# x of the first two tiles split by partitions over two queues, the K weights on ScalarE's queue, and new orders on all engines

## The chip, the cores and the metric

The kernel runs on one core of a Trainium2 chip. Its time is the device time of that core in microseconds (us); the time of a kernel is the median of its runs. A profile is one profiled execution. Engines: PE is TensorE (matmuls; PEld its weight loads), DVE is VectorE, ACT is ScalarE, POOL is GpSimd, SP is SyncE, which here only issues transfers. ACT issues a few transfers too.

## What is computed

A linear-attention block and a gated feed-forward block, each behind a layer norm and with a residual; 2048 rows of width 448, 16 heads of 28, feed-forward width 1792, bf16.

```python
def _A_ref(x, wqkv, wo):
    qkv = (x @ wqkv) ...            # q, k, v of 16 heads of 28
    phi = lambda t: jnp.where(t > 0, t + 1, jnp.exp(t)) + 1e-6
    pq, pk = phi(q), phi(k)
    kv = jnp.einsum("bhsd,bhse->bhde", pk, v)
    z = jnp.einsum("bhsd->bhd", pk)
    num = jnp.einsum("bhqd,bhde->bhqe", pq, kv)
    den = jnp.einsum("bhqd,bhd->bhq", pq, z)[..., None] + 1e-6
    return (num / den) ... @ wo

def _B_ref(x, w_gate, w_up, w_down):
    g = jnp.einsum("bsd,df->bsf", x, w_gate)
    u = jnp.einsum("bsd,df->bsf", x, w_up)
    return jnp.einsum("bsf,fd->bsd", _gelu(g) * u, w_down)

h = x + _A_ref(_layernorm(x), A_wqkv, A_wo)
h2 = h + _B_ref(_layernorm(h), B_w_gate, B_w_up, B_w_down)
```

## The kernel before

The 2048 rows lie in SBUF as 16 tiles of 128: partition p holds rows 16p to 16p+15, tile t is row 16p+t of each (`xv`). So neighbouring tiles of one partition lie side by side in memory.

**Head and K stage.** For each tile DVE takes the statistics (`bnst1_t`, line 413, and `bnag1_t`, line 414), ACT a logarithm and an exponential (`ln1_t`, line 420, and `rstd1_t`, line 422: the reciprocal root of the variance). Tiles 0 to 3 are normalized on DVE (`normD_t`, line 435), transposed on PE (`tr0_t` and `tr1_t`, line 443, two blocks each), and copied back by ACT (`evxA_t`, line 448) and DVE (`evxD_t`, line 450). Tiles 4 to 15 are normalized on POOL (`negm1_t`, `normP_t`, line 453) and transposed by a transfer that SP issues (`xT_t`, line 455). Then PE makes the K tiles and the Q tiles (`k_t`, `q_t`, line 469: four matmuls of 448 columns each, the third and fourth of which also need `dw0_t` or `dw1_t`, the last 64 rows of the weights), ACT and DVE make phi of K (`ek_t`, `ck_t`, `pk_t`, lines 480 to 482), and PE adds pk^T times the normalized rows over all tiles in four banks (`pt...`, line 488; the last columns of xnn hold ones and give z). Before any of this PE runs `warm`: WARM matmuls of 128 columns on a constant (line 407).

**Middle.** The sums in the banks are copied out (lines 514 to 521), multiplied by the V weights (`kv`, line 527), masked to heads, multiplied by wo (`w2_c`, line 547). The remaining Q tiles fill PE meanwhile. Per pair of tiles the denominator is formed (`cq`, `aq`, `t1`, `dr`, `rd`, `pn`, lines 564 to 593), the result is transposed (`tro` on PE for the first pair, `oT_p` as transfers) and multiplied (`out...`), x is added (`hr_t`, line 633), and the second layer norm follows (`nhP_t` on POOL, `wrap_t` on DVE, line 664, and the transfer `hT_t`, line 665).

**Gate and up stage.** In chunks of 2, 2, 4, 4 and 4 tiles PE makes gate and up products (`gu2_v`, `gu4_v`, lines 731 and 733) into a ring of two banks each; ACT takes the gelu (`ge0_v`, `ge1_v`, line 751), DVE the product (`hm0_v`, `hm1_v`, line 753); a unit v+2 needs both products of unit v. The down products (`downA_p`, `downB_p`, line 697; `down448_14`, `down224_15`, line 678) are placed between the units, DVE adds x (`fo...`) and SP stores (`do_t`).

**What sets the order.** Every operation is a task with a number, in the order in which the builder makes it. The order of each engine is written out by hand in `ORDERS`: five lists of task numbers for PE, ACT, DVE, POOL and SP. An engine works strictly along its list. Waits follow from what a task reads and writes. Where a task waits for more than one semaphore, all but the last wait are instructions of their own ahead of it; `HOLD` names, for a task, whose wait stands first. It has 15 entries.

The first transfers are issued in this order: on SP x of tile 0, x of tiles 2 and 3, `dw1` (Q weights, 384 rows), x of tiles 4 to 7, `dw1_t`, the rest of x, then V weights and wo; on ACT x of tile 1, `dw0` (K weights, 384 rows), `dw0_t` (K weights, the last 64 rows), and then the table load `tbl1`.

Of the kernel before, what the change touches and what calls it, by code (L numbers as in the profile page):

```python
# [48 lines left out]
)  # L49
HOLD = {  # L50
    66: (36,), 141: (140,), 165: (164,), 214: (213,), 216: (215,), 323: (302,), 326: (324,), 431: (340,), 704:
    (564,), 735: (734,), 781: (672,), 839: (836,), 849: (846,), 854: (852,), 866: (865,),
}


class _Buf:
    __slots__ = ("name", "writer", "readers")

    def __init__(self, name):
        self.name = name  # L60
        self.writer = None
        self.readers = []

# [165 lines left out]
def bass_sequential_preLN__linear_attn_block__glu_gated_geglu__prompt_kernel(  # L229
# [13 lines left out]
    WARM = 40  # L243
# [579 lines left out]
```

## Time and profile before

| | |
|---|---|
| median of 3 runs | 190.3 us (190.28 to 190.66) |
| span of the profiled execution, first to last instruction | 188.3 us |
| the profiled execution's own time | not recorded; the median is 2.0 us over the span |
| PE busy | 184.3 us (98%) |
| DVE busy | 129.3 us (69%) |
| ACT busy | 76.5 us (41%) |
| POOL busy | 50.0 us (27%) |
| transposes xT, issue to landing | 2.5 to 4.1 us, median 2.7 us |

Busy time is the union of an engine's instructions. The chain of waits follows the work that ended last back through what released it; 94% of it is PE, 3% DVE, 1% transfers. Times inside the span count from its first instruction. An issue row on SPq or ACTq is the time the queue's engine spends on issuing; the landing time is counted from the start of that issue. In a row "L469 PE MATMUL ps<-wqk_sb,xnT ... x8" eight instructions of line 469 that follow each other are merged, with the start of the first and the time to the end of the last.

### The profile page before, as it was taken

Reading aid. Unit: us, or ns where it says so; the run is one execution under the profiler, and the core shown is the slowest. Engines: PE = TensorE matmul, PEld = TensorE weight load, DVE = VectorE, ACT = ScalarE, POOL = GpSimd, SP = SyncE. Lnnn points to the kernel's source line nnn. Section 1 sums busy time; section 2 is a strip of 40 time slices with the busy share of each in tenths; the row PEclk is TensorE's granted clock in tenths of the full one; section 3 lists DMA queues with packets and bytes.
Section 4 is the critical chain, followed back from the end, with each engine's and each line's share of the span. In section 5 each row is a group of like instructions: output and inputs, shape, how many; then the busy total and the mean of one; then the engine's idle time right before and its main releaser. Section 6 shows DMA issues by size and latency. Waiting matters only on the chain.

```text
span 188.3 us, 4459 instructions
## 1 busy us (share of the span) xinstructions
PE 184.3 (98%) x1813; PEld 109.2 (58%) x1813; DVE 129.3 (69%) x330; ACT 76.5 (41%) x220; POOL 50.0 (27%) x91
## 2 busy tenths in 40 slices
PE   7999999999999999999999999999999999999994
PEld 7545555555688788965554555555545545454554
DVE  4999959999899998786796762562645244335432
ACT  3878752799963231432234222321242222224100
POOL 6067910704505686033614000206100000000000
PEclk9999999999999999999999999999999999999999
DMA  5996458999393526820005720000096000002024
GB/s 169 387 231 88 96 104 194 218 222 174 65 320 64 95 52 116 84 52 0 0 3 98 144 54 0 0 3 2 3 135 111 3 0 24 3 0 98 3 79 140
DMA packets 35076, 17.11 MB, mean 91 GB/s; under 512 B 26864, under 2 KB 33648, under 8 KB 35056
## 3 DMA queue, kind: packets, MB, share of 16 engines
q1 hardware_dynamic: 34432, 16.32, 41.1%
q10 hardware_dynamic: 624, 0.52, 0.8%
q8 instruction: 14, 0.23, 0.5%
q14 instruction: 6, 0.05, 0.1%
HBM read 8.26 MB, written 1.84 MB: 54 GB/s over the span
## 4 chain that ended last, share of the span: by engine, by line
PE 94%; DVE 3%; DMA 1%; issue 0%
PE ps L733 38%; PE ps L697 19%; PE ps L469 12%; PE ps L731 9%; PE ps L488 6%; PE ps L627 3%; PE ps L678 3%; PE ps L628 2%; DMA x_sb<-in_A_x_dram 1%; DVE st L413 1%; PE ps L617 1%; PE ps L547 1%; PE ps L527 1%; PE ps L443 0%; PE ps L654 0%; DVE den L572 0%
## 5 line engine op out<-in xcount | busy, mean ns | idle before, releaser
L733 PE MATMUL ps<-hnT,wgu_sb 64*128 64x512 bf16 (+1 forms) x490 | 88.8, 333 | 0.0
L731 PE MATMUL ps<-hnT,wgu_sb 64*128 64x512 bf16 (+1 forms) x490 | 88.6, 333 | 0.0
L751 ACT ACTIVATE gl<-ps 128x256 bf16<-128x256 f32 x112 | 36.6, 383 | 85.3 <-PE ps L731 84.4
L753 DVE TENSOR_TENSOR hh<-ps,gl 128x256 bf16<-128x256 f32 x112 | 42.1, 416 | 41.4 <-ACT gl L751 41.3
L733 PEld LDWEIGHTS ps<-hnT,wgu_sb 64*128 64x128 bf16 x490 | 45.2, 94 | 32.9 <-DVE hh L753 3.4
L731 PEld LDWEIGHTS ps<-hnT,wgu_sb 64*128 64x128 bf16 x490 | 45.4, 94 | 2.5
L697 PE MATMUL ps<-wd_sb,hh 64*128 64x448 bf16 x392 | 41.5, 349 | 0.0
L697 PEld LDWEIGHTS ps<-wd_sb,hh 64*128 64x128 bf16 x392 | 23.2, 94 | 14.5
L469 PE MATMUL ps<-wqk_sb,xnT 128*128 128x448 bf16 x128 | 27.4, 353 | 0.0
L413 DVE BATCH_NORM_STATS2 st<-x_sb 128x6 f32<-128x448 bf16 x32 | 19.2, 612 | 1.8 <-DMA x_sb<-in_A_x_dram 1.7
L585 POOL TENSOR_TENSOR t<-pq,zbc 128x448 f32<-128x448 bf16 x12 | 12.3, 1042 | 23.7 <-DVE pq L583 22.0
L469 PEld LDWEIGHTS ps<-wqk_sb,xnT 128*128 128x128 bf16 x128 | 11.9, 98 | 11.4 <-DVE pk L482 0.8
L488 PE MATMUL ps<-pk,xnn 128*128 128x448 bf16 x64 | 13.9, 352 | 0.0
L627 PE MATMUL ps<-w,pqnT 64*128 64x448 bf16 x49 | 11.5, 349 | 0.1
L425 POOL TENSOR_SCALAR ln<-mv 128x2 f32<-128x2 f32 x7 | 2.0, 291 | 35.2 <-DVE mv L414 35.0
L480 ACT ACTIVATE e<-ps 128x448 bf16<-128x448 f32 x16 | 8.5, 539 | 5.6 <-PE ps L469 5.5
L628 PE MATMUL ps<-pt_sb,pqnT 64*128 64x448 bf16 x42 | 10.2, 350 | 0.0
L633 DVE TENSOR_TENSOR x_sb<-ps,x_sb 128x448 bf16<-128x448 f32 x16 | 9.6, 616 | 0.7 <-PE ps L628 0.6
L662 POOL TENSOR_SCALAR hn<-x_sb,nm,rs 128x448 bf16<-128x448 bf16 x14 | 9.9, 719 | 0.4
L482 DVE SCALAR_TENSOR_TENSOR pk<-ps,e 128x448 bf16<-128x448 f32 x16 | 9.8, 617 | 0.1
L488 PEld LDWEIGHTS ps<-pk,xnn 128*128 128x128 bf16 x64 | 6.3, 98 | 5.9 <-DVE pk L482 0.3
L453 POOL TENSOR_SCALAR xnn<-x_sb,nm,rs 128x448 bf16<-128x448 bf16 x12 | 8.9, 744 | 2.2 <-ACT rs L422 1.9
(85 smaller groups left out, 160.5 us busy)
## 6 DMA issues: line engine op xcount, KB each, us to landing
out_dram<-x_sb SPq DMA_DIRECT2D x15, 112.0 KB, 1.8
wd_sb<-in_B_w_down_dram SPq DMA_DIRECT2D x1, 1568.0 KB, 8.4
x_sb<-in_A_x_dram SPq DMA_DIRECT2D x3, 448.0 KB, 5.9
wgu_sb<-in_B_w_gate_dram SPq DMA_DIRECT2D x1, 896.0 KB, 12.1
wgu_sb<-in_B_w_up_dram SPq DMA_DIRECT2D x1, 896.0 KB, 16.5
wgu_sb<-in_B_w_gate_dram SPq DMA_DIRECT2D x1, 672.0 KB, 6.1
wgu_sb<-in_B_w_up_dram SPq DMA_DIRECT2D x1, 672.0 KB, 8.5
wo_sb<-in_A_wo_dram SPq DMA_DIRECT2D x1, 392.0 KB, 7.5
```

What stands on the lines that cost most here:

```text
L413: op("dve", lambda e: e.bn_stats(st[:, t, :], src_ap), [b_src], [b_st[t]], "bnst%s_%d" % (tag, t))
L469: ins = e.matmul(ps[:, bk, 0:D], xnT[:, t, k, :], wqk_sb[:, k, c0:c0 + D], start=(k == 0), stop=(k == 3))
L488: ins = e.matmul(ps[:, BK_PT[c], 0:D], xnn[:, t % XN_R, c * 128:(c + 1) * 128], pk[:, ip, :], start=(t == 0), stop=(t == T - 1))
L585: op("pool", lambda e, n=n: e.tensor_tensor(t1[:, n, :], pq[:, a + n, :], zbc[:, :], ALU.mult), [b_pq[a + n]] + b_z, [b_t1[n]], "t1p_%d" % ...
L627: e.matmul(ps[:, BK_OUT[0], 0:D], pqnT[ra, i2, sg // 2, :], w2[ra, sg // 2, :], start=(sg == 0), stop=(sg == 5))
L628: ins = e.matmul(ps[:, BK_OUT[1], 0:D], pqnT[rb, i2, 3 + (sg + 1) // 2, :], (w2 if sg == 6 else w2s)[rb, sg // 2, :], start=(sg == 0), sto ...
L662: op("pool", lambda e, t=t, sh=sh: e.tensor_scalar(hn[:, sh, 0:D], x_sb[:, t, :], nm2[:, t:t + 1], rs2[:, t:t + 1], ALU.add, ALU.mult), [b ...
L697: ins = e.matmul(ps[:, bko[half][n], 0:D], hh[rows, j, sl[n]], wd_sb[rows, j, :], start=(j == 0 and (half == 0 or p == 6)), stop=(j == NJ ...
L731: first = e.matmul(psG[:, jj * N:(jj + 1) * N], wgu_sb[A_, k, j * 128:(j + 1) * 128], hnT[A_, ka_, c0:c0 + N], start=(k == 0), stop=(k == ...
L733: ins = e.matmul(psU[:, jj * N:(jj + 1) * N], wgu_sb[B_, k, j * 128:(j + 1) * 128], hnT[B_, kb_, c0:c0 + N], start=(k == 0), stop=(k == NK ...
L751: G.add("act", lambda e, gi=gi, cs_=cs_, psG=psG: e.activation(gl[:, gi, cs_], psG[:, cs_], AF.Gelu_apprx_tanh), r=[b_ps[BK_G[i]]], w=[b_g ...
L753: op("dve", lambda e, dst=dst, srcU=srcU, srcL=srcL: e.tensor_tensor(dst, srcU, srcL, ALU.mult), [b_ps[BK_U[i]], b_glh], [b_ar[j_][t % HR] ...
```

## The change

1. x of tiles 0 and 1 is loaded as one array, split by partitions: partitions 0 to 63 on SP's queue, 64 to 127 on ACT's. The statistics of tiles 0 and 1 wait for both halves.
2. SP then issues `dw0_t`, x of tiles 2 and 3, x of tiles 4 to 7, `dw1_t` and the rest; ACT issues `dw0` and `dw1`, and then the table load.
3. WARM goes from 40 to 36.
4. All five orders are new, and `HOLD` has an entry for nearly every task with a wait.

```diff
-    WARM = 40
+    WARM = 36
...
-        dma_x("sp", 0, 1)
-        dma_x("act", 1, 2)
+        x01 = [dma(q, x_sb[rows, 0:2, :], xv[rows, 0:2, :], b_, "dx0%s" % "ab"[i]) for i, (q, rows, b_) in enumerate((("sp", A_, b_x[0:2]), ("act", B_, [_Buf("x01")])))]
+        dma_w1("sp", wqk_sb, D, 2 * D, b_wk, "dw0_t")
+        dma_w3("act", wqk_sb, D, 2 * D, b_wk, "dw0")
         dma_x("sp", 2, 4)
-        dma_w3("act", wqk_sb, D, 2 * D, b_wk, "dw0")
-        tx1 = dma_w1("act", wqk_sb, D, 2 * D, b_wk, "dw0_t")
-        dma_w3("sp", wqk_sb, 0, D, b_wq, "dw1")
+        tx1 = dma_w3("act", wqk_sb, 0, D, b_wq, "dw1")
         dma_x("sp", 4, 8)
...
         def ln_stats(t, src_ap, b_src, st, mv, b_st, b_mv, tag):
-            op("dve", lambda e: e.bn_stats(st[:, t, :], src_ap), [b_src], [b_st[t]], "bnst%s_%d" % (tag, t))
+            G.add("dve", lambda e: e.bn_stats(st[:, t, :], src_ap), r=[b_src], w=[b_st[t]], name="bnst%s_%d" % (tag, t), sync=x01[1:] if tag == "1" and t < 2 else ())
```

The orders are lists of hundreds of numbers; written as names, these are the places that the prediction speaks of (each list goes on):

```
DVE  before  wvpad wqkpad bnst1_0 bnag1_0 bnst1_1 bnag1_1 normD_0 bnst1_2 normD_1 bnag1_2 bnst1_3 evxD_0 ...
DVE  after   wqkpad bnst1_0 bnst1_1 bnag1_0 wvpad bnag1_1 bnst1_2 normD_0 bnag1_2 normD_1 bnst1_3 evxD_0 ...
PE   before  ... k_1 q_0 tr0_3 tr1_3 k_2 k_3 pt4_0 q_1 pt4_1 pt4_2 q_2 k_4 pt4_3 k_5 q_3 k_6 pt4_4 k_8 pt4_5 k_7 pt4_6 k_10 k_9 ...
PE   after   ... k_1 tr0_3 tr1_3 q_0 k_2 k_3 pt4_0 pt4_1 q_1 k_4 q_2 q_3 pt4_2 k_5 pt4_3 k_6 k_7 pt4_4 pt4_5 k_8 k_9 k_10 ...
ACT  before  ... ln1_8 ek_3 eq_0 ln1_7 rstd1_8 rstd1_7 ...
ACT  after   ... ek_3 ln1_8 rstd1_8 eq_1 rq_1 ln1_7 rstd1_7 ...
PE   before  ... pt1_14 pt1_15 pt3_13 pt3_14 pt3_15 q_5 q_4 kv ...
PE   after   ... pt1_15 pt3_12 pt3_13 pt3_14 pt3_15 q_4 q_5 kv ...
DVE  before  ... evpD_3 z0 aq_1 t1d_0 dr_0 evpD_2 rd_0 ...
DVE  after   ... evpD_3 z0 t1d_0 dr_0 dr_1 evpD_2 ...
DVE  after   ... hm1_9 hm0_9 fo448_0 wrap_7 cqP_6 wrap_4 rdP_5 ...
SP   before  ... hT_4 oT_4 hT_5 hT_7 hT_6 oT_5 ...
SP   after   ... oT_4 hT_5 hT_6 hT_7 hT_4 oT_5 ...
PE   after   ... downB_6 down224_15 down448_14 down224_15
```

POOL's order puts `ident`, `kvzpad` and `ones2` ahead of `eps`, and several other constants behind the first normalizations. Between gate and up units the down products, `fo448`, `wrap` and the stores stand in other places.

More of the change, by code (lines that the diff above doesn't have):

```diff
@@ L15 @@
 ORDERS = (
[33 rows of a table removed]
[33 rows of a table added]
 )
 HOLD = {
-    66: (36,), 141: (140,), 165: (164,), 214: (213,), 216: (215,), 323: (302,), 326: (324,), 431: (340,), 704:
-    (564,), 735: (734,), 781: (672,), 839: (836,), 849: (846,), 854: (852,), 866: (865,),
[77 rows of a table added]
 }
```

143 rows, old and new, of tables (HOLD, ORDERS) are left out of this document.

## The prediction

> **What bounds the kernel now.** I read the page's totals first, then the list of waits of PE, then the chain of waits over the first 16 us.
>
> ```profile
> span 188.3 us, 4459 instructions
> PE 184.3 (98%) x1813; PEld 109.2 (58%) x1813; DVE 129.3 (69%) x330; ACT 76.5 (41%) x220; POOL 50.0 (27%) x91
> ...
> PE ps L443 <- DVE xnn L435: 0.4, 1, 0.4
> ...
> 0.79 2.53 DMA x_sb<-in_A_x_dram
> ...
> 3.34 0.64 DVE st L413
> ...
> 6.09 0.40 PE ps L443 x4
> ...
> 6.88 0.55 PE ps L469 x2
> ...
> 7.65 1.51 PE ps L469 x8
> ```
>
> The span is 188.3 us and the median of the runs 190.3, so 2.0 us lie outside the profiled instructions; I keep them and add the sum to 190.3. Between its first real work and the last 2 us of the span PE is at work: after the warm-up it waits in the list of PE once, for 0.4 us. So nothing on DVE, ACT, POOL or the queues is worth time except what lets PE begin sooner (x lands, DVE takes statistics and normalizes, PE transposes, K0) or closes a small hole. On the other side, anything that comes late for PE is paid in full. The eight matmuls at 7.65 take 1.51 us; a unit of four (one K tile, one Q tile, one "pt" product) is 0.757 us.
>
> **Part 1: the head.** Transfers and issues in the order of landing times and of the queues, then DVE's steps:
>
> ```profile
> x_sb<-in_A_x_dram SPq DMA_DIRECT2D x1, 112.0 KB, 2.5
> x_sb<-in_A_x_dram ACTq DMA_DIRECT2D x1, 112.0 KB, 2.7
> x_sb<-in_A_x_dram SPq DMA_DIRECT2D x1, 224.0 KB, 3.4
> wqk_sb<-in_A_wqkv_dram ACTq DMA_DIRECT2D x1, 336.0 KB, 4.2
> ...
> 0.79 0.87 SPq L346 DMA_DIRECT2D x_sb<-in_A_x_dram  x2
> 1.25 1.01 ACTq L346 DMA_DIRECT2D wqk_sb<-in_A_wqkv_dram  x2
> 1.71 0.43 SPq L346 DMA_DIRECT2D wqk_sb<-in_A_wqkv_dram  x1
> ...
> 4.10 0.59 DVE L413 BATCH_NORM_STATS2 st<-x_sb 128x6 f32<-128x448 bf16 x1
> 4.22 0.29 ACT L420 ACTIVATE ln<-mv,eps_t 128x1 f32<-128x1 f32 x1 [0.65 <-DVE mv L414]
> 4.83 0.36 DVE L435 TENSOR_SCALAR xnn<-x_sb,mv,rs 128x448 bf16<-128x448 bf16 x1
> 5.11 0.62 DVE L413 BATCH_NORM_STATS2 st<-x_sb 128x6 f32<-128x448 bf16 x1
> 6.54 0.27 DVE L450 COPY xnT<-ps 128x256 bf16<-128x256 bf16 x1
> ```
>
> Each half of the new array has the 112 KB of one old tile, in half as many rows of twice the length. Statistics of tile 0 started with tile 0's landing (0.79 + 2.5, at 3.34); now they need both halves. The nearest rows are those two transfers: 2.5 and 2.7 us. Bounds for the start: 3.1 (longer rows gain 0.2) to 3.6; I take the slower old queue, 0.80 + 2.7 = 3.5, which is +0.1 rounded down. Behind the waiting instruction stand all of DVE's head, and through it ACT's logarithms and PE's transposes.
>
> DVE's new order takes both tiles' statistics, then tile 2's, before it normalizes tile 0. Up to the copy of line 450 that releases the second half of K0 (6.54, which is 3.20 after 3.34) the same statistics, aggregates and normalizations stand in another order, plus the pad of wv_sb moved in, about 0.15. The gaps that the old order left for ACT are used, so I count the order itself at nothing (0 to +0.15). But statistics of tile 2 now stand in front of tile 0's normalization, and x of tiles 2 and 3 became the third issue of SP instead of the second: 1.71 instead of about 1.22 (two issues take 0.87). With the old 3.4 us it lands at 5.1; if the engines serve the K weights first (1.25 + 4.2) at 5.45; if it has them to itself at the old 4.6. DVE gets there at 3.45 + two statistics, two aggregates and the pad (0.53 + 0.53 + 0.35) = 4.86. The wait is 0 to 0.6; I take 0.2, the row of the same transfer. Everything behind it on DVE moves with it. Head: +0.1 + 0.2 = **+0.3** (-0.2 to +0.8).
>
> [...]
>
> Priced at nothing: ACT issues three transfers as before, and the logarithm waited 0.65 for DVE, which covers a table load that comes up to that much later; beyond it each 0.1 costs 0.1. The four warm-up matmuls fewer end the warm-up earlier, and the transpose waits for DVE in any case (rival 3 has the other side). POOL's small constants move behind its pads and are needed only at 4.22.
>
> **Part 2: K tiles come earlier on PE.** The new PE order takes K4 two units sooner (before q_2, with pt4_1 ahead of q_1) and K7 three units sooner (straight behind K6). Both read transposes that SP issues one after the other.
>
> ```profile
> L455 SPq DMA_TRANSPOSE xnT<-xnn x1: 1307/1307/1307, 10.3 to 10.3; - x1
> DMA to landing us min/median/max: 3.3/3.3/3.3
> L455 SPq DMA_TRANSPOSE xnT<-xnn x1: 1264/1264/1264, 16.6 to 16.6; - x1
> ...
> 13.80 1.68 PE L469 MATMUL ps<-wqk_sb,xnT 128*128 128x448 bf16 x8
> 20.61 0.92 PE L469 MATMUL ps<-wqk_sb,xnT 128*128 128x448 bf16 x4
> ...
> 13.88 0.33 ACT L422 ACTIVATE rs<-ln 128x1 f32<-128x1 f32 x2
> 14.17 0.75 POOL L453 TENSOR_SCALAR xnn<-x_sb,nm,rs 128x448 bf16<-128x448 bf16 x1 [0.23 <-ACT rs L422]
> ```
>
> The rows at 13.80 are q_2 and K4, so K4 starts at 14.55; two units sooner is 13.04. Its transpose, issued at 10.3, lands 3.3 later: 13.6. K4 would be 0.55 late. K7 is the row at 20.61; three units sooner is 18.34. Its transpose (the row at 16.6, also 3.3) lands at 19.95: 1.6 late, and the 0.55 is part of that. That is the upper bound, with all transposes as before. For the lower: ACT's new order takes the reciprocal root of tile 8 directly behind its logarithm; before, it stood behind two exponentials and came at 13.88, which held POOL (14.17), and with it tile 8's and then tile 7's transpose. That can bring K7's transpose 0.4 to 0.85 forward, so K7 is 0.75 to 1.2 late with a landing of 3.3; with the quickest landing of this list, 2.5, it is on time. Bounds 0 to 1.6; I take **+0.8**. A head that is late moves both sides alike and adds to this. K9 and K13 also stand two units sooner, but their lateness is inside the same slip.
>
> **Part 3: the kv product.** Here a hole can close.
>
> ```profile
> 32.73 0.62 DVE pt_sb L516
> 33.79 0.39 DVE pq L565
> 34.76 0.62 DVE den L572
> ...
> 34.23 1.68 PE L469 MATMUL ps<-wqk_sb,xnT 128*128 128x448 bf16 x8
> 35.96 1.03 PE L527 MATMUL ps<-pt_sb,wv_sb 128*112 128x112 bf16 x16
> ```
>
> Two Q tiles from 34.23 take 1.51, to 35.74; kv starts at 35.96: a hole of 0.22. The chain to it on DVE loses the 0.39 (done earlier now) and gains a second reduction of 0.6: +0.2. But pt1_15, which starts that chain, has twelve instead of nine matmuls behind it, 3 x 0.189 = 0.57 more cover. The hole goes: **-0.2** (-0.22 to 0).
>
> **Part 4: the gate and up stage.** The same tight ring of two banks remains.
>
> ```profile
> PEld ps L733 <- DVE hh L753: 3.4, 12, 0.4
> ...
> L665 SPq DMA_TRANSPOSE hnT<-hn x2: 1221/1282/1343, 73.7 to 74.9; - x2
> DMA to landing us min/median/max: 4.5/4.7/4.9
> 81.00 0.19 PE ps L731
> ```
>
> Twelve times weights wait for DVE's product and PE just does not. DVE's inserted operations (fo448, wrap, hr) are moved between such places, not added, so nothing by itself, with PE's own queue as cover; where one falls into a run of units it costs up to 0.3. The new HOLD table only changes which of several waits stands in front; no row shows its price. A few hundredths at twelve such places bound it by +0.4, and since PE starves nowhere here, nothing can be gained; I take 0. Transposes of hn: the last of tiles 4 to 7 was issued at 74.9 and landed 4.9 later, at 79.8, for the unit that begins just before 81.00. Now tile 4's copy stands behind fo448_0, wrap_7 and cqP_6, so the last issue is near 77: with 3.0 to 4.9 it lands 0.8 early to 1.1 late. I take **+0.1** (0 to 1.1), nearer to the early end because the other hn transposes mostly take 3. The stores moved on SP and the new order of the last three products hide behind the remaining matmuls: 0.
>
> **Sum.** 190.3 + 0.3 + 0.8 - 0.2 + 0.1 = **191.3 us**.
>
> **Rivals.** 1, faster: x lands much sooner as 1792-byte rows. Place: the first statistics; price: each 0.1 before 3.34. At a start of 2.9 PE starts 0.45 sooner, the kv hole gives 0.2, and if the K transposes then meet their units the time is 189.7. It becomes faster than before from a start of about 3.1 with part 2 at nothing. For it: the shorter warm-up fits such a start, and the row length doubles; against it: 2.5 and 2.7 us for the same bytes, and two queues that must both finish.
>
> 2, no change: the head costs 0.3, the kv hole pays 0.2, and the transposes are as early as their units: 190.4. For it speaks the one landing of 2.5 in that list; against it K7's three units.
>
> 3, the clock stays low:
>
> ```profile
> 1.05 4.43 PE L407 MATMUL ps<-ones_bf 128*128 128x128 bf16 x40 [1.05 <-POOL eps_d L383]
> 47.69 0.94 PE L654 MATMUL ps<-ident,hn 128*128 128x128 bf16 x14
> ...
> PEclk9999999999999999999999999999999999999999
> ```
>
> Forty 128-column matmuls took 4.43 us, fourteen took 0.94 later: PE ran at half rate (0.107 against 0.056 us each) until the transposes began, though the page's clock row reads 9 throughout. With 36 the run ends 0.43 sooner and PE then idles for a microsecond or so. If the full rate needs another 4.2 us of work from there, half of that is lost: 190.3 + 2.1 + 0.3 - 0.2 = 192.5 before part 2. [...]
>
> **How the numbers follow.** Forecast 0.53 (190.7 to 192.4 by its bounds), rival 1 0.24, rival 2 0.17, rival 3 0.06. Slower by over 0.2% (about what a measurement of this kernel can tell from no change, 0.38 us): 0.53 + 0.06 = 0.59; within: 0.17; faster: 0.24. The range runs from 189.8 to 192.4; it leaves out the better half of rival 1 and most of rival 3. The forecast's own range is 190.7 to 192.4.
>
> **What would show it.** Statistics of tile 0 near 3.45 and of tile 2 only after a wait for x; the first transposes near 5.6 to 6; PE waiting before K4 and above all before K7 for xnT; no hole before L527. A first statistics row before 3.0, or K4 and K7 that start without a wait, would prove me wrong.

## The result and the profile after

The changed kernel runs in 197.75 us (median of 4 runs, 197.61 to 198.14), the kernel before beside it in 190.32 (190.28 to 190.66): ratio 1.0384 [1.0364, 1.0404], **7.3 us slower**. The prediction said 191.3 and ended its range at 192.4: right in sign, far too small.

The page of the changed kernel, total and clock. PE is busy for 1.9 us more and stands still for 5.5 us more. The clock row has something new in its second and third digits.

```profile
span 195.7 us, 4458 instructions
PE 186.2 (95%) x1809; PEld 129.9 (66%) x1809; DVE 130.0 (66%) x330; ACT 76.3 (39%) x220; POOL 50.6 (26%) x91
...
PEclk9879999999999999999999999999999999999999
```

The list of waits of PE (us in total, times, longest). Before, it held one wait for work, 0.4 us for the transposes; the row L481 is the start of the warm-up and stood there too.

```profile
PE ps L517 <- DVE xnn L509: 2.6, 1, 2.6
PE ps L543 <- DMA xnT<-xnn: 1.5, 1, 1.5
PE ps L481 <- POOL ones_bf L453: 1.0, 1, 1.0
PE ps L701 <- DMA pqnT<-pqn: 1.0, 1, 1.0
PE ps L805 <- issue: 0.8, 1, 0.8
```

Four waits, at four places: the transposes of tile 0 (line 517), K7 (543), the `out` product of pair 2 (701) and the first gate product of tiles 8 to 11 (805). Lines count differently in each kernel; 74 more stand ahead of PE's work here than before.

The chain of waits over the first 45 us (start, us, what) shows the first two and the kv product:

```profile
0.78 0.59 SPq L421
...
1.44 0.83 SPq L421
...
2.32 4.33 DMA x_sb<-in_A_x_dram
...
6.68 0.63 DVE st L487
7.30 0.29 DVE xnn L509
...
8.51 1.65 PE ps L543 x4
...
19.95 3.58 DMA xnT<-xnn
...
23.57 0.93 PE ps L543 x4
...
38.53 1.48 POOL t L643
40.03 0.62 DVE den L646
40.65 0.54 DVE pt_sb L595
41.20 0.04 issue
41.24 1.03 PE ps L601 x16
```

At 2.32 SP issues x of tiles 2 and 3, as its third transfer. It lands 4.33 us later, DVE takes the statistics of tile 2 at 6.68, and only behind these it normalizes tile 0 (7.30). PE transposes at 7.66 instead of 5.29. K0 (8.51) takes 1.65 us for four matmuls that take 0.93 at 23.57. The landings of x (last number: us from issue):

```profile
x_sb<-in_A_x_dram SPq DMA_DIRECT2D x1, 224.0 KB, 4.3
...
x_sb<-in_A_x_dram SPq DMA_DIRECT2D x1, 112.0 KB, 3.2
x_sb<-in_A_x_dram ACTq DMA_DIRECT2D x1, 112.0 KB, 2.5
```

The slow matmuls are a matter of the clock. The table of windows (window, length; busy us and instructions of PE, PEld, DVE, ACT, POOL; granted clock of PE; DMA share; GB/s):

```profile
4.93:8.35 3.42, 0.83 (x10) 0.45 (x8) 2.53 (x9) 1.62 (x7) 0.00 (x0) 1.00 1.06 368
8.35:11.76 3.41, 3.33 (x14) 1.59 (x13) 2.84 (x12) 1.78 (x7) 0.24 (x1) 0.50 1.06 356
```

From 8.35 to 11.76, for 3.41 us, PE has half the clock (0.50). In the 3.42 us ahead of it PE had worked for 0.83 us only. The other three executions of this kernel took as long; two show the same clock (0.991 over the run), and the longest reads 1.00, so what its head did stays open. The last two columns show the 16 DMA engines full from 4.93 to 11.76 (share 1.06). They are as full in the kernel before (1.06 from 5.33 to 8.74); what differs is which transfers go ahead of x of tiles 2 and 3.

The third wait, in the chain and in the timeline of DVE (the timeline's columns: start, us, engine, line, operation):

```profile
53.67 1.00 DVE pqn L664
...
54.69 4.86 DMA pqnT<-pqn
```
```profile
50.45 0.66 DVE L656 TENSOR_SCALAR eq<-eq 128x896 bf16<-128x896 bf16 x2
...
53.10 0.56 DVE L657 TENSOR_TENSOR pq<-pq,eq 128x896 bf16<-128x896 bf16 x1
53.58 1.08 DVE L664 TENSOR_TENSOR pqn<-pq,rd 128x896 bf16<-128x896 bf16 x1
```

`pnP_2` (53.58) feeds the transfer `oT_2`. The new order puts `cqP_4`, `cqP_3` (50.45) and `aqP_3` (53.10) ahead of it: three operations for later pairs, about 1.1 us. The transfer goes out at 54.69, lands 4.86 later, and PE has been waiting since 58.6. The order alone does not make the wait: five of the seven `oT` transfers of this trace land after 2.9 to 3.2 us, and with 3.0 this one would have been there at 57.7, before PE asked. The fourth wait, in the timeline of SP:

```profile
109.65 4.87 SPq L739 DMA_TRANSPOSE hnT<-hn  x3
114.56 0.58 SPq L782 DMA_DIRECT2D out_dram<-x_sb  x1
115.19 1.23 SPq L739 DMA_TRANSPOSE hnT<-hn  x1
```

`hT_9` (115.19) is issued behind `hT_10`, `hT_11`, `hT_8` and the store `do_3`. The down product ends at 119.34, and PE waits 0.79 us for this transfer, though the list of waits names it "issue". Here too the landing has its part: 4.7 us, where the three `hnT` issued ahead of it took 2.9 to 3.0.

Where the 7.4 us between the two spans lie, by the start of five pieces of PE's work in the traces:

| | K2 | kv | first gate | gate of tiles 4 to 7 | end of PE |
|---|---|---|---|---|---|
| before | 9.22 | 35.96 | 50.14 | 80.81 | 185.86 |
| after | 12.80 | 41.24 | 55.42 | 87.37 | 193.29 |
| added in the stretch | +3.6 | +1.7 | 0.0 | +1.3 | +0.9 |

### The profile page after: what moved, and what is told of

It reads as the page before. It is cut to its first block, busy times and chain, and to the rows that moved or that the text cites. A ratio compares the mean times of both kernels' runs of the same rounds, so it can differ in the third digit from the quotient of the medians.

```text
span 195.7 us, 4458 instructions
## 1 busy us (share of the span) xinstructions
PE 186.2 (95%) x1809; PEld 129.9 (66%) x1809; DVE 130.0 (66%) x330; ACT 76.3 (39%) x220; POOL 50.6 (26%) x91
## 3 DMA queue, kind: packets, MB, share of 16 engines
HBM read 8.26 MB, written 1.84 MB: 52 GB/s over the span
## 4 chain that ended last, share of the span: by engine, by line
PE 82%; DMA 7%; DVE 6%; POOL 1%; ACT 1%; issue 1%; SPq 1%
PE ps L805 31%; PE ps L771 19%; PE ps L807 11%; PE ps L543 8%; PE ps L562 4%; PE ps L752 3%; DMA pqnT<-pqn 2%; PE ps L701 2%; DMA x_sb<-in_A_x_dram 2%; DMA xnT<-xnn 2%; PE ps L702 2%; DVE st L487 1%; POOL t L643 1%; SPq L421 1%; PE ps L621 1%
## 5 line engine op out<-in xcount | busy, mean ns | idle before, releaser
L827 DVE TENSOR_TENSOR hh<-ps,gl 128x256 bf16<-128x256 f32 x112 | 42.9, 416 | 41.0 <-ACT gl L825 40.7
L771 PE MATMUL ps<-wd_sb,hh 64*128 64x448 bf16 x392 | 40.0, 349 | 0.0
L771 PEld LDWEIGHTS ps<-wd_sb,hh 64*128 64x128 bf16 x392 | 29.0, 94 | 8.5
L543 PE MATMUL ps<-wqk_sb,xnT 128*128 128x448 bf16 x128 | 28.1, 365 | 1.6 <-DMA xnT<-xnn 1.5
L543 PEld LDWEIGHTS ps<-wqk_sb,xnT 128*128 128x128 bf16 x128 | 12.5, 100 | 13.3 <-DMA xnT<-xnn 2.0
L659 POOL TENSOR_TENSOR t<-pq,zbc 128x448 f32<-128x448 bf16 x12 | 13.9, 1178 | 21.3 <-DVE pq L657 21.3
L562 PE MATMUL ps<-pk,xnn 128*128 128x448 bf16 x64 | 13.3, 352 | 0.0
L491 POOL TENSOR_SCALAR nm<-mv 128x1 f32<-128x1 f32 (+1 forms) x19 | 4.1, 222 | 35.0 <-DVE mv L488 34.3
```

Source lines behind the costliest of these rows:

```text
L543: ins = e.matmul(ps[:, bk, 0:D], xnT[:, t, k, :], wqk_sb[:, k, c0:c0 + D], start=(k == 0), stop=(k == 3))
L562: ins = e.matmul(ps[:, BK_PT[c], 0:D], xnn[:, t % XN_R, c * 128:(c + 1) * 128], pk[:, ip, :], start=(t == 0), stop=(t == T - 1))
L659: op("pool", lambda e, n=n: e.tensor_tensor(t1[:, n, :], pq[:, a + n, :], zbc[:, :], ALU.mult), [b_pq[a + n]] + b_z, [b_t1[n]], "t1p_%d" % ...
L771: ins = e.matmul(ps[:, bko[half][n], 0:D], hh[rows, j, sl[n]], wd_sb[rows, j, :], start=(j == 0 and (half == 0 or p == 6)), stop=(j == NJ ...
L827: op("dve", lambda e, dst=dst, srcU=srcU, srcL=srcL: e.tensor_tensor(dst, srcU, srcL, ALU.mult), [b_ps[BK_U[i]], b_glh], [b_ar[j_][t % HR] ...
```

## The experiments

Theory: the loss has three causes that can be parted. (a) x of tiles 2 and 3 comes late, because a transfer with half the partitions and the small weights stand ahead of it; PE's pause is then followed by half the clock (0.50 from 8.35 to 11.76). (b) K4 and above all K7 stand too early. (c) Two transposing transfers are released late in the new later orders. Rival: the orders cost little, and what the trace shows behind the head only follows from the late head. Comparisons are with the kernel before in the same set of runs (190.3 to 190.9).

### The transfers alone, the orders alone, the warm-up, the split

**The transfers alone.** The kernel before with the new transfers and nothing else.

```diff
-        dma_x("sp", 0, 1)
-        dma_x("act", 1, 2)
+        x01 = [dma(q, x_sb[rows, 0:2, :], xv[rows, 0:2, :], b_, ...)  # partitions 0-63 on sp, 64-127 on act
+        dma_w1("sp", wqk_sb, D, 2 * D, b_wk, "dw0_t")
+        dma_w3("act", wqk_sb, D, 2 * D, b_wk, "dw0")
         dma_x("sp", 2, 4)
...
-        dma_w3("sp", wqk_sb, 0, D, b_wq, "dw1")
+        tx1 = dma_w3("act", wqk_sb, 0, D, b_wq, "dw1")
```

> The kernel before with the new first transfers alone (x of two tiles split by partitions, K weights' last rows third in the list of SP's work, Q weights on ACT); its orders, HOLD and 40 warm-up matmuls stay. Theory A (the new transfers make the late head): first statistics near 4.1 instead of 3.34, tile 2's not before 6.6, the second pair of transposes near 7.5 instead of 6.09, and PE then at half rate for a window, so 192.5 to 194. Theory B (the new orders make the loss, transfers are nearly free): within 0.5 us of 190.3.

Measured: 194.1 us, ratio 1.0194 [1.0129, 1.0259]: half of the loss. Its chain:

```profile
2.31 5.44 DMA x_sb<-in_A_x_dram
...
7.77 0.63 DVE st L384
```

K2 starts at 13.40, 4.2 us late, and all that follows runs as before (K2 to kv 26.71 us; before, 26.74).

**The orders alone.** The changed kernel with the transfers and the 40 warm-ups of before.

```diff
-    WARM = 36
+    WARM = 40
...
-        x01 = [dma(q, x_sb[rows, 0:2, :], ...
+        dma_x("sp", 0, 1)
+        dma_x("act", 1, 2)
...
```

> The changed kernel with the old first transfers and 40 warm-up matmuls: the new orders and the new HOLD alone. Theory A (head from the transfers, and apart from it the three later waits of PE, before K7 1.7, before outA_2 1.1 and before gu4_28 1.0, from the orders themselves): head within 0.3 of the kernel before, the three waits still there, 193.5 to 194.5. Theory B' (the later waits are only the echo of the late head): 190 to 191, no wait before K7.

Measured: 194.56 us, ratio 1.0231 [1.0174, 1.0288]. So the orders cost something without the late head, and the rival falls. In the profiled execution one transposing transfer, K4's, was slow:

```profile
11.00 5.19 DMA xnT<-xnn
```

PE waited 2.1 us for it, and half rate followed from 17.02 to 20.44 (clock 0.50). That execution is the longest of the four, 196.65. The other three took 194.3 to 194.8, and their clock reads full throughout. So by the clock the half rate belongs to that one execution, and without it the orders cost about 3.9. The two cuts by stages below, with the old HOLD, find 1.0 to 1.2 and 1.6 of it; no trace shows the remaining 1.2 or so.

**Warm-up of 80.** The changed kernel with PE kept at work until the transposes.

```diff
-    WARM = 36
+    WARM = 80
```

> The changed kernel with 80 warm-up matmuls instead of 36, so that PE has work until about 7.6. Clock theory (the pause from 4.9 to 7.66 cost PE its full rate from 8.35 to 11.76): K0 and K1 at 0.76 us each, no 577 ns matmuls, 1.2 to 1.5 us less than the changed kernel, about 196.3. Rival (the half rate comes at its own time and has nothing to do with the pause): 197.7, K0 still slow.

Measured: 195.55 us, ratio 1.0264 [1.0239, 1.0288]: 2.2 us less than the changed kernel, though the transposes come later (8.36). The clock stays full:

```profile
4.14:7.55 3.41, 3.00 (x53) 2.83 (x51) 1.83 (x6) 0.99 (x4) 0.00 (x0) 1.00 1.06 365
7.55:10.96 3.41, 2.52 (x21) 1.50 (x22) 3.29 (x12) 2.38 (x8) 0.00 (x0) 1.00 1.01 378
```

K0 to K2 takes 2.71 us instead of 4.29: at full rate this stretch is 1.6 shorter. But K0 starts 0.70 later (9.21), so K2 is only 0.9 earlier. Another 0.45 lies between K2 and kv, and 0.8 behind the gate of tiles 4 to 7, where the wait for `hT_9` (0.8 in the changed kernel) is missing. So the half rate is a cause with a price of its own, 1.6 us; the 2.2 are not all its doing. In these two traces it goes with a PE that does little ahead of it: busy for 0.83 us of 3.42 in the changed kernel, for 3.00 and 2.52 of 3.41 here.

**Whole tiles again.** The changed kernel with x of tile 0 on SP and of tile 1 on ACT, all other transfers in their new places.

```diff
-        x01 = [dma(q, x_sb[rows, 0:2, :], xv[rows, 0:2, :], b_, ...
+        dma_x("sp", 0, 1)
+        dma_x("act", 1, 2)
```

> The changed kernel with x of tiles 0 and 1 loaded as two whole tiles on the two queues again, all other transfers in the new places and both tiles' statistics still waiting for both. Theory A1 (splitting by partitions itself is slow on SP's queue): first statistics at 3.5 instead of 4.13, x of tile 2 lands 0.2 to 0.6 earlier than 6.65, 0.3 to 1.0 us less, more if the clock window is missed no longer. Rival A2 (only the place in the queue counts): first statistics near 4.1 all the same, 197.7.

Measured: 198.37 us, ratio 1.0419 [1.0356, 1.0481], not faster than the changed kernel. Statistics began at 3.48 instead of 4.13, but x of tiles 2 and 3 landed at 6.5 as before (4.7 us from its issue), and tile 0's normalization stands behind it. Inside the changed kernel the split is covered by the late x2 (x of tiles 2 and 3).

### The late orders

**Late orders alone.** The kernel before, with the new orders only from the first gate products on (transfers, K stage, HOLD old).

```diff
 each engine's list
-old                                   | old
+old, up to the first gate products    | new
```

> The kernel before, with the new orders only from the first gate unit on (PE behind outB_1, ACT behind tbl2, DVE behind bnag2_0, POOL behind pow2_2, SP behind oT_2); old transfers, old head and K stage, old HOLD. Theory C (the late orders hold waits of their own: before outA_2, because DVE does cqP_4, cqP_3 and aqP_3 ahead of pnP_2, about 1.0; before gu4_28, because hT_9 is issued behind hT_11, hT_8 and a store, 0.2 to 1.0): 191.5 to 192.5 with these two waits. Rival C' (those waits were the echo of the late head): 190.2 to 190.6, none of them.

Measured: 192.53 us, ratio 1.0085 [1.0064, 1.0107], 1.6 us slower, with both late transfers in the list of waits of PE:

```profile
PE ps L599 <- DMA pqnT<-pqn: 0.9, 1, 0.9
PE ps L703 <- issue: 0.5, 1, 0.5
```

**The same, with the two transfers released sooner.**

```diff
 DVE
-... cqP_4 cqP_3 drP_2 nhD_1 nhD_0 wr64_1 wr64_0 rdP_2 aqP_3 pnP_2 ...
+... drP_2 nhD_1 nhD_0 wr64_1 wr64_0 rdP_2 pnP_2 cqP_4 cqP_3 aqP_3 ...
 SP
-... hT_10 hT_11 hT_8 do_3 hT_9 ...
+... hT_10 hT_9 hT_11 hT_8 do_3 ...
```

> late_new with two moves: on DVE cqP_4, cqP_3 and aqP_3 go behind pnP_2, and on SP hT_9 goes ahead of hT_11 and hT_8 (the store do_3 behind them). Theory C: both waits go, 190.2 to 190.6. Rival (the transposes themselves land late, whatever the order): the waits shrink by less than half, 191 to 192.

Measured: 190.82 us, ratio 0.9996 [0.9982, 1.0010]. Both waits are gone, and with them the whole cost. It need not be the order alone, though: `oT_2` landed 2.96 us after its issue in the kernel before and 4.86 in the changed kernel, where with 2.96 PE would not have waited for it (57.65 against 58.6). The lists of waits do not part the two. What stands beside the slow landings is told in the last section. What is left of "issue" is 0.2 us in the list, in front of the first gate product of tiles 4 to 7, where `hT_4` is issued last of four.

**That last wait.** As before it, and `hT_4` issued second of the four, with `nhP_4` on POOL and `wrap_4` on DVE moved up for it.

```diff
 POOL
-... nhP_5 t1p_11 t1p_10 ... nhP_7 nhP_6 nhP_4 ...
+... nhP_5 nhP_4 t1p_11 t1p_10 ... nhP_7 nhP_6 ...
 DVE
-... wrap_5 hm1_7 ... wrap_7 cqP_6 wrap_4 ...
+... wrap_5 wrap_4 hm1_7 ... wrap_7 cqP_6 ...
 SP
-... hT_5 hT_6 hT_7 hT_4 ...
+... hT_5 hT_4 hT_6 hT_7 ...
```

> The kernel before with the new late orders and the two mended waits, and besides hT_4 issued as the second of the four (with nhP_4 and wrap_4 moved up on POOL and DVE). If the 0.4 us left in front of the first gate product of tiles 4 to 7 comes from hT_4 being issued last: 190.2 to 190.5, the wait gone, level with or 0.2 under the kernel before. If it comes from the four transfers as a whole: the wait stays and the time is 190.8.

Measured: 191.52 us, ratio 1.0049 [1.0035, 1.0063]: a miss. The wait at tiles 4 to 7 is gone, so it was `hT_4`; but a new one came, 0.6 us for a product of DVE, some 9 us earlier. The timelines of DVE of the kernel before it and of this one:

```profile
69.59 1.32 DVE L562 TENSOR_TENSOR pqn<-pq,rd 128x896 bf16<-128x896 bf16 x1
```
```profile
69.81 2.01 DVE L562 TENSOR_TENSOR pqn<-pq,rd 128x896 bf16<-128x896 bf16 x1
```

The same product took 1.32 us there and 2.01 here (1.08 to 1.09 for all six of this size in the kernel before). Why it took longer these two timelines do not show; the one of 1.32 in the changed kernel, with two products of POOL beside it, is in the last section. By the two traces the edit bought 0.4 us and paid 0.75; the median is 0.7 over `late_fix`, so part of it is open.

**HOLD alone.** The kernel before with the new HOLD table.

```diff
-HOLD = {...}   # 15 entries
+HOLD = {...}   # nearly every task with a wait
```

> The kernel before with the new HOLD table alone: for nearly every task the wait that is released last stands in front as an instruction of its own. If the extra step behind the late wait costs a few hundredths at the places where a product of DVE comes just in time for the gate and up units: 190.5 to 191.0. If it costs nothing that PE sees: 190.2 to 190.5.

Measured: 190.69 us, ratio 0.9994 [0.9981, 1.0007]. The table costs nothing under the old orders; under the new ones it was not parted. (In this profile one transposing transfer made PE wait 0.4 us; the list of the kernel before has no wait for a transfer.)

**The kv product.** The kernel before with the copy that kv needs (`evpD_2`) ahead of the reduction `dr_0`.

```diff
-... aq_1 t1d_0 dr_0 evpD_2 rd_0 ...
+... aq_1 t1d_0 evpD_2 dr_0 rd_0 ...
```

> The kernel before with one move: on DVE the copy evpD_2 (line 521), the last one that kv waits for, goes ahead of the reduction dr_0. If the hole of 0.22 before kv hangs on that chain alone, kv starts right behind q_4 and 0.2 us are won: 190.1. If the denominators of the first pair, which now come 0.54 later, are the next to be late (tro_0, out1): no gain or a loss of up to 0.3.

Measured: 190.75 us, ratio 0.9992 [0.9981, 1.0003]. The hole in front of kv closed, and PE lost 0.16 between q_7 and q_8 and 0.19 in front of a transpose instead. The hole was not worth 0.2 us.

### What of the transfers

Two halves of the transfers' change, each in the kernel before: **the split alone** (x2 second on SP, the weights where they were), and **the places alone** (whole tiles; `dw0_t` ahead of x2 on SP, `dw1` on ACT).

```diff
 the split alone
-        dma_x("sp", 0, 1)
-        dma_x("act", 1, 2)
+        x01 = [dma(q, x_sb[rows, 0:2, :], xv[rows, 0:2, :], b_, ...
```

> The kernel before with x of tiles 0 and 1 split by partitions over the two queues and both statistics waiting for both halves; every other transfer stays in its queue and place (x of tiles 2 and 3 second on SP), all orders old. Theory 1 (the split costs only its own lateness): the halves land at 3.9 to 4.0 and 3.4 us, first statistics at 4.0, first transpose at 5.9 instead of 5.3, x of tiles 2 and 3 lands by 5.3, no wait of PE over 0.7 us, granted clock full from the end of the warm-up on: +0.5 to +0.8 us. Theory 2 (the split alone already makes the long pause of PE, by delaying everything issued behind it): x of tiles 2 and 3 lands after 6.3, PE waits over 2 us, a window at half rate follows, +2.5 to +4 us.

```diff
 the places alone
+        dma_w1("sp", wqk_sb, D, 2 * D, b_wk, "dw0_t")
         dma_x("sp", 2, 4)
-        tx1 = dma_w1("act", wqk_sb, D, 2 * D, b_wk, "dw0_t")
-        dma_w3("sp", wqk_sb, 0, D, b_wq, "dw1")
+        tx1 = dma_w3("act", wqk_sb, 0, D, b_wq, "dw1")
```

> The kernel before with whole tiles of x as before, but the small K-weight transfer ahead of x of tiles 2 and 3 on SP, and the Q weights on ACT; all orders old. Theory 1 (the place of x of tiles 2 and 3 makes the pause): first statistics at 3.4, first transpose at 5.3 as before, x of tiles 2 and 3 lands at 6.3 to 7.5, statistics of tile 2 hold normalization of tile 1, PE waits 1.5 to 3 us between the transposes of tile 0 and the rest, and half rate follows if the wait is over 2 us: +1.5 to +3.5 us. Theory 2 (the split makes it): x of tiles 2 and 3 lands by 5.3, +0 to +0.5 us.

Measured: the split 191.57 us, ratio 1.0062 [1.0032, 1.0093]; the places 193.54 us, ratio 1.0145 [1.0113, 1.0178]. 1.2 and 2.8 us: together 3.9, and the two at once cost 3.7. Both theories had a part of it, the places the larger. The landing of x2 in their chains, the split first:

```profile
1.43 4.35 DMA x_sb<-in_A_x_dram
```
```profile
1.87 5.78 DMA x_sb<-in_A_x_dram
```

Before, it was issued at 1.24 and landed 3.4 us later. Issued 0.6 us later, it lands 3.0 us later than before (7.65 against 4.6). In the changed kernel, which has the same places, the K weights land at 5.2 and 5.3, in the kernel before at 5.4 and 6.8: they go ahead of it now, where it went ahead of them. The two transfers newly ahead of x2 have 56 and 336 KB, 1.1 us at the 372 GB/s that the trace of the places has from 6.31 to 9.73; with the 0.6 of the issue that estimate has 1.7 of the 3.0. Part of the rest is scatter: with all the new transfers x2 landed at 6.65 in the changed kernel and at 7.75 in the kernel with the transfers alone. In the profile of the split PE never waited over 1.0 us and the clock stayed full; two of its ten executions read 0.991, and they are the two slowest (192.74, 193.31). With the places alone all four read 0.991, and in the profile eight matmuls of K and Q tiles from 10.34 took 3.06 us, where eight took 1.68 with the split alone (8.19): half the clock is part of the 2.8.

### The K stage

**PE's new K order alone,** in the kernel before, and **the changed kernel with PE's old K order,** old transfers and the two late transfers mended.

```diff
 the first: PE of the kernel before
-... k_3 pt4_0 q_1 pt4_1 pt4_2 q_2 k_4 pt4_3 k_5 q_3 k_6 pt4_4 k_8 pt4_5 k_7 ...
+... k_3 pt4_0 pt4_1 q_1 k_4 q_2 q_3 pt4_2 k_5 pt4_3 k_6 k_7 pt4_4 pt4_5 k_8 ...
 the second: the reverse in the changed kernel
```

> The kernel before with only PE's order up to the K tile of tile 15 exchanged for the new one (K4 two units sooner, K7 straight behind K6). By the bounds of the prediction: K4 0.55 late, K7 0.75 to 1.6 late, less what Q tiles cover: +0.8 with bounds 0 to 1.6 us. If the new order costs nothing by itself and the 1.7 us of the changed kernel come from its late head: +0 to +0.2. If a transpose lands as late as 5 us after its issue (as in the kernel with the new orders alone): PE waits over 2 us, half rate follows, +3 us or more.

> The changed kernel with the transfers and the warm-up of before, PE's K stage in the order of before, the three DVE products (cqP_4, cqP_3, aqP_3) put behind pnP_2, and hT_9 issued ahead of hT_11, hT_8 and do_3. If the named pieces (transfers, K stage, the two late transposes) are the whole cost of the change, it is within 0.5 us of the kernel before (190.5 to 191.2), with the gap at the kv product and 0.2 to 0.4 at the gate and up units of tiles 4 to 7 left. If some further part of the new ACT, DVE or POOL orders costs, it is over 191.5.

Measured: 193.72 us, ratio 1.0164 [1.0141, 1.0186], and 199.24 us, ratio 1.0451 [1.0399, 1.0504]. By their numbers they fall into the dearest of the expected cases, but not by the waits foreseen there: PE does not wait for transfers, and neither run answers the question. Their waits of PE:

```profile
PE ps L441 <- ACT eq L468: 1.5, 2, 1.0
...
PE ps L441 <- DVE pk L454: 0.6, 1, 0.6
```
```profile
PE ps L535 <- DVE pk L529: 4.4, 3, 2.6
```

PE's order is paired with those of ACT and DVE, which empty its banks and make pk. With one side exchanged alone, PE waits for products that the other side makes later. I had built a mismatch and measured it.

**All five orders new up to kv,** transfers and later orders old, is the sound cut.

```diff
 each engine's list
-old               | old
+new, up to kv     | old
```

> The kernel before (its transfers, WARM 40, HOLD) with the new orders of all five engines from the start up to the product kv and the old orders behind it. Theory 1 (early and late costs add): the kernel with all new orders and old transfers was at 194.6 and the one with only the late orders 1.6 us over the kernel before, so this one is at 192.4 to 193.2, with the wait at K4 (0.5 to 2.3 us) and perhaps half rate behind it. Theory 2 (the early orders cost nothing by themselves, the wait at K4 was one late landing): 190.5 to 191.2.

Measured: 191.71 us, ratio 1.0052 [1.0033, 1.0071]: 1.0 to 1.2 us. Between the two theories: K4's landing of 5.2 us was one late case, but the early orders do cost. Its waits of PE:

```profile
PE ps L415 <- DVE xnn L407: 0.6, 1, 0.6
PE ps L441 <- DMA xnT<-xnn: 0.4, 1, 0.4
```

K2 is 0.25 late, K2 to kv takes 27.30 instead of 26.74 (K4's wait), and another 0.4 lies at the seam to the old orders. K7 has no wait here.

**K7 back.** The changed kernel with K7 behind K8, on PE, ACT and DVE alike.

```diff
 PE
-... k_6 k_7 pt4_4 pt4_5 k_8 k_9 ...
+... k_6 pt4_4 pt4_5 k_8 k_7 k_9 ...
 ACT
-... ek_6 ek_7 ln1_14 ... ek_8 ek_9 ...
+... ek_6 ln1_14 ... ek_8 ek_7 ek_9 ...
 DVE
-... ck_7 ck_6 cq_2 ... pk_6 pk_7 ck_9 pk_9 aq_3 ck_10 ck_8 pk_8 ...
+... ck_6 cq_2 ... pk_6 ck_8 pk_8 ck_7 pk_7 ck_9 pk_9 aq_3 ck_10 ...
```

> The changed kernel with one thing undone: K7 comes behind pt4_4, pt4_5 and K8 again, with its exponential and products on ACT and DVE behind those of K8. If the 1.7 us wait of PE in front of K7 is a price of its early place: -1.2 to -1.7 us against the changed kernel, 196.0 to 196.6. If it is given back at the next wait (the copy of the last sums, kv): within 0.3 of the changed kernel, 197.5 to 198.0.

Measured: 197.40 us, ratio 1.0347 [1.0322, 1.0371]; the changed kernel is at 1.0384 [1.0364, 1.0404]. The wait for K7's transpose is gone, but the gain is 0.4 us by the medians and 0.7 by the ratios, with intervals that just touch, not 1.2 to 1.7. K2 to kv went from 28.44 to 27.57; new waits for pk came at K9 and K11. So less than half of the 1.7 us came back.

**All named waits mended** in the changed kernel: the edit of K7 back, and that of the two late transfers on DVE and SP.

> The changed kernel with three things undone: K7 as in the run beside it, the three DVE products behind pnP_2, and hT_9 issued ahead of hT_11, hT_8 and do_3. What is left of the change then is its transfers and warm-up. If the named waits are the whole cost of the orders: 194.0 to 194.9, that is the time of the kernel before with the new transfers alone (194.1) and up to 0.7 for the small gaps. If some unnamed part of the orders costs: over 195.3.

Measured: 195.56 us, ratio 1.0275 [1.0222, 1.0327]; the two late transfers are worth 1.8 us here, as in the kernel before. It is just over my limit of 195.3: one unnamed part shows in the list of waits, at the first gate product,

```profile
PE ps L777 <- DVE hnT L706: 0.5, 1, 0.5
```

where a copy of DVE (the first hnT) is late. Of the 5 us that remain over the kernel before, 3.7 are the transfers by their own run; 0.7 lie at this product, 0.6 at K11, 0.4 at the gate products of tiles 4 to 7.

### The head

**40 warm-ups** in the changed kernel, and **tile 0 first**: the normalizations of tiles 0 and 1 ahead of the statistics of tile 2 on DVE.

```diff
-    WARM = 36
+    WARM = 40
```

> The changed kernel with WARM 40 instead of 36. The warm-up ends 0.43 us later, so PE's pause in front of the first transpose is 2.1 to 2.3 instead of 2.6 us. If the half rate behind it comes from any pause of this size (the kernel with the new transfers alone had 40 warm-ups and half rate): within 0.4 us of the changed kernel, 197.3 to 198.1. If the four matmuls decide it: no window at half rate, 1.4 to 2.2 us less, 195.5 to 196.4.

```diff
 DVE
-... bnag1_1 bnst1_2 normD_0 bnag1_2 normD_1 bnst1_3 evxD_0 ...
+... bnag1_1 normD_0 normD_1 bnst1_2 evxD_0 bnag1_2 bnst1_3 ...
```

> The changed kernel with DVE's head order turned back in one place: the normalizations of tiles 0 and 1 stand ahead of the statistics of tile 2, and the copy of tile 0 right behind these. If most of the head's loss comes from the statistics of tile 2 (which wait for x until 6.6) holding back tile 0: first transpose at 6.2 to 6.4 instead of 7.7, K0 at 7.5 to 7.9 instead of 8.5, the pause of PE split in pieces of about 1.2 us, no half rate or less of it: 1.0 to 2.2 us less than the changed kernel. If the late x decides by itself (K1 waits for tile 2 in any case): PE's wait moves from the first transpose to K1, 0 to 0.6 us less.

Measured: 197.57 us, ratio 1.0368 [1.0351, 1.0385], and 197.95 us, ratio 1.0377 [1.0362, 1.0393]: neither differs from the changed kernel. The four warm-ups are free. With tile 0 first the transposes begin at 6.39 instead of 7.66, but K2 at 12.84 instead of 12.80:

```profile
PE ps L489 <- DVE xnn L481: 1.5, 2, 1.3
...
PE ps L515 <- ACT rs L468: 1.1, 1, 1.1
```

The pause comes in three pieces, the last of them because ACT's new order has tile 2's logarithm ahead of tile 0's copy, and the half rate stays (0.50 from 8.84 to 12.25).

## Why the prediction was wrong

**The sign was right, the sum was not.** By separate runs the parts are: transfers +3.7 (ratio 1.0194 [1.0129, 1.0259]), and all orders with the new HOLD about +3.9. That is 7.6, the whole 7.3 within the noise. Of the orders' 3.9 the cuts name the early ones with 1.0 to 1.2 and the late ones with 1.6; HOLD is 0 under the old orders. About 1.2 us stay open.

**Part 1, +0.3: the step that failed most.** At the copy that releases the second half of K0 the head is 1.89 us late (6.54 before, now line 524 at 8.43), where 0.3 was priced:

```profile
6.68 0.63 DVE L487 BATCH_NORM_STATS2 st<-x_sb 128x6 f32<-128x448 bf16 x1 [0.75 <-DMA x_sb<-in_A_x_dram]
...
8.43 0.28 DVE L524 COPY xnT<-ps 128x256 bf16<-128x256 bf16 x1
```

0.79 is the later start of statistics (4.13 instead of 3.34; priced at 0.1), 0.75 DVE's wait for x2 (priced at 0.2), and the remaining 0.35 the order with the pad (priced at 0 to 0.15). The half rate behind it adds about 1.6, so K2 is 3.6 late. The sum left the half rate out, as a rival. The start of statistics was to be at 3.5; it came at 4.13, because the half on SP landed 3.2 us after its issue (I had taken 2.5 to 2.7 from whole tiles). The split costs 1.2 us, not 0.1. And the wait for x2 was to be 0.2, at most 0.6: x2 was to land by 5.45; it landed at 6.65, and at 7.65 with the places alone. It was to be issued at 1.71; the two issues ahead of it took 0.59 and 0.83 us, and it went out at 2.32. And I had set its landing by the K weights at the latest, with no room for Q weights beside it. Where I wrote that the order itself costs nothing I had noted that tile 2's statistics stand in front of tile 0; turning that back alone changes nothing (`norm_first`): a wait for tile 2 then sits in the queues of ACT and PE.

The redistribution freed nothing: while x2 is under way, from 2.32 to 6.65, the trace has the DMA engines full (share 1.02, 328 GB/s). And the two halves were no gain: they landed after 3.2 and 2.5 us, the two whole tiles before after 2.5 and 2.7.

**Rival 3, chance 0.06: it happened,** in the way named (PE waits 2.6 us for the transposes, and the clock is at 0.50 from 8.35 to 11.76), with the wrong trigger. I tied it to the 36 warm-ups; with 40 the profiled execution reads the same clock (0.991). What goes with it is the late x. Its price was put at 2.1; K0 to K2 at full rate is 1.6 us shorter (2.71 us with 80 warm-ups, 4.29 here).

**Part 2, +0.8: mechanism right, the number partly by luck.** It lies close to the 1.0 to 1.2 of the early orders, but K7, most of the 0.8, is not in those. K4: 0.55 late by the prediction, 0.56 measured in the stretch K2 to kv of the early orders alone. K7: none there, 1.7 in the changed kernel (the upper bound was 1.6), of which undoing it returned 0.4 to 0.7. ACT's earlier root of tile 8 did not help K7 in the changed kernel: the issue of tile 8's transpose on SP took 2.17 us (median 1.26), so K7's went out at 19.95, and it landed 3.58 us later.

**Part 3, -0.2: wrong.** The hole stayed: the chain shows POOL's product at 38.53 with 1.48 us, behind which the reduction at 40.03 and the copy wait. I had counted DVE's two operations and not POOL's. And the experiment in the kernel before shows that the hole was worth nothing.

**Part 4, +0.1: the right place was priced, the wrong ones were missed.** The transposes of tiles 4 to 7 cost 0.15, and HOLD 0 under the old orders. But I had followed only those four transfers. `oT_2` (PE waits 1.0 us, and 0.9 with the late orders alone) and `hT_9` (0.8 and 0.5) stood in lists that I had read for other names, the first behind three operations of DVE, the second behind `hT_10`, `hT_11`, `hT_8` and the store `do_3`; together they are most of the 1.6 us of the late orders. Both needed the late issue and a slow landing: 4.9 and 4.7 us, where 3.0 would have been in time.

## What to carry to other kernels

Before moving a transfer back in its queue, add up the bytes of all queues that now go ahead of it: here 0.6 us of issue became 3 us of landing, and the bytes newly ahead are, by estimate, 1.1 of it. For an engine without slack, follow every transposing transfer of the new order from the operation that releases it to the product that needs it, once with a landing of 3 us and once with 5 (2.9 to 5.05 us is what those of `hn` and `pqn` took in the traces of the two kernels): two missed ones cost more than all that was priced. To test an order, cut all engines at the same seam; a single engine's list in another kernel measures a mismatch.

## What the runs showed of the hardware

**Half the clock, and how long PE was busy ahead of it.** In three profiles the whole of it was read: half the clock (0.50) lasted 3.41 us in the changed kernel (8.35 to 11.76) and with tile 0 first (8.84 to 12.25), and 3.42 with the orders alone (17.02 to 20.44). The 3.4 us ahead of it in the last two, and for contrast a stretch of that length with the split alone, behind which the clock stayed at 1.00 for the next 3.41 us:

```profile
5.43:8.84 3.41, 1.18 (x11) 0.68 (x12) 3.13 (x11) 2.03 (x9) 0.00 (x0) 1.00 1.04 362
```
```profile
13.60:17.02 3.42, 1.27 (x8) 0.47 (x7) 3.42 (x12) 1.95 (x7) 2.69 (x8) 1.00 1.16 86
```
```profile
3.96:7.37 3.41, 1.84 (x25) 1.25 (x22) 3.29 (x10) 1.86 (x8) 0.00 (x0) 1.00 1.05 370
```

PE busy for 0.83 us (the changed kernel), 1.18 and 1.27 us was followed by half the clock; 1.84 us (the split alone) and 3.00 and 2.52 us (80 warm-ups) were not. With tile 0 first no single pause in the head was over 1.3 us, while a wait of 2.6 us in the K stage, in the changed kernel with PE's old K order, was followed by eight matmuls in 1.53 us (26.58), with the clock at 1.00 in every stretch of 2 us from 20 to 34. What sets the clock no run shows.

**A product of POOL beside one of DVE.** In the changed kernel `pnP_2` (53.58, on DVE) took 1.08 us, and the product t of POOL that began beside it at 53.75 took 1.82. The product `pqn` at 75.47 took 1.32 us on DVE; of the two products t beside it, the first (74.81) took 1.04 and the second (75.80) 1.89. The four other `pqn` of this size, with no product t beside them, took 1.07 to 1.08, and eleven of the fifteen products t 1.03 to 1.04. This is read from the overlap in one trace; no run parts it further.

**Landings of the transposing transfers, and the packets of another queue.** In the traces of the kernel before and of the changed kernel, 14 of the 24 transfers of `xnn` landed 2.4 to 2.7 us after their issue, the others after 2.9 to 4.1. Of the 42 of `hn` and `pqn`, 30 landed after 2.9 to 3.2 us and 12 after 3.7 to 5.05. Both pages list a queue called "instruction" with 14 packets (0.23 MB, 16 KB each). For `oT_2` such a packet begins 2.84 us behind the issue in the changed kernel (57.53), and the landing took 4.86; in the kernel before it begins 4.77 us behind (53.07), and the landing took 2.96. In the five cases of these two traces in which a packet begins 0.9 to 2.2 us behind the issue of an `hn` or `pqn` transfer, the landing took 4.1 to 4.9 us; in the six with one 2.3 to 2.9 us behind, four took 4.7 to 4.9 and two 2.9 and 3.0. With none from 1 us before the issue to 5 us behind it, 18 of 19 landed after 2.9 to 3.1 us and one after 3.7. So the order on DVE may have cost PE its wait by moving the issue up against a packet. No run moved the packet alone: the two go together, and the cause is not shown.
